# Loading the gathers' block numbers into registers for several query blocks at once

## The chip, the cores and the metric

One core of one Trainium2 chip. The metric is the device time of one execution of the kernel in microseconds. Three runs of the kernel before took 892.53, 896.0 and 898.25 us, median 896.0 us.

## What is computed

Block-sparse attention and, on its result, a bilinear feed-forward layer. There are 4 batches of 8 heads, 768 positions, head width 64. Positions form 24 blocks of 32. A query block attends to its two neighbours and itself, to block 0, to block 23 and to three sampled blocks; query blocks 0 and 23 attend to everything.

```python
scores = scale * np.matmul(q, k.transpose(0, 1, 3, 2))
...
for qb in range(n_blocks):
    for kb in sampled_blocks[qb]:
        mask[qb * block:(qb + 1) * block, kb * block:(kb + 1) * block] = True
scores = np.where(mask, scores, -1000000000.0)
...
return (a * b @ w_out).astype(np.float32)   # a = x @ w_a, b = x @ w_b
```

The sampled block numbers are an input (24 x 3 integers), so the kernel reads them at run time.

## The kernel before

**Tiling.** The 3072 tokens form 12 chunks of 256 (three for each batch; the first batch takes its middle chunk first, so its order of query blocks is 8 to 15, 0 to 7, 16 to 23). Each chunk has 8 query blocks. Of 96 query blocks 88 are sparse (1 to 22 of each batch) and 8 are dense (0 and 23). For a sparse one TensorE forms scores against 8 gathered key blocks (lines 976 and 875, tile `s`), VectorE finds the maximum (line 991), ScalarE the exponentials (line 1001, tile `sm`), both split the result into two half-precision parts (lines 893 to 900, tile `hl`), SyncE's queue transposes those by DMA (line 1023; line 1118 for dense ones; tile `pt`), and TensorE multiplies by the gathered values (line 919, tile `av`). When all 8 blocks of a chunk are done and scaled (lines 1163 and 1166, tile `xT`), the chunk goes through the feed-forward layer: first products `ab` (line 1202, 24 matmuls of 128x256 a step, 12 steps a chunk), their product and its split (lines 1219 to 1249), second products `o` (lines 1283 to 1285). The weights are unpacked and split during the first part of the span, by VectorE (lines 727 to 768) and ScalarE.

**The gathers.** For a sparse query block keys come by GpSimd copies inside the on-chip memory (`gather_keys`): one copy of the three neighbour blocks (line 586), now and then two of the blocks 0 and 23, and three copies of 128x128 words at offsets held in registers (line 591), into one of two buffers `KG`. Values come by DMAs on SyncE's queue (`gather_values`): one of three blocks (line 621), now and then two more (lines 623, 624), and three whose source address is held in a register (line 626), into one of two buffers `VG`. The offsets were clamped and multiplied by VectorE into two small tables, `offs` for values and `offs_k` for keys (lines 424 to 433). Ahead of the three register-addressed operations of every sparse query block, `dynamic` (line 563) loads that block's three offsets from the table into three registers of the queue that will use them. It is one instruction, TENSOR_LOAD, at line 566, on SyncE's queue for values and on GpSimd's queue for keys.

**What sets the order.** Every engine runs its instructions in program order, and that order is fixed when the kernel is built, by a planner in the kernel's own code (class `Plan`). Each piece of work is a generator that yields steps with an engine, a cost in ns and a rank; the planner keeps the time at which each engine, the DMA queue and the descriptor generator come free by these costs, and issues the step that can begin first, weighed by rank (attention by its query block, weights from 8 on, the feed-forward layer 8000 and more, so it fills). A step of `gather_values` costs SyncE 3000 ns in the plan, 1250 ns more with the two extra DMAs, 475 ns for a dense block (line 631). For a step with its last field set, as this one, the planner also holds the descriptor generator for the step's cost (line 159), and loads on ScalarE's queue wait for that one too. A step of `gather_keys` costs GpSimd 2000 ns (line 595). Nothing on the chip rereads these costs: they act only through the order of each engine's program.

Of the kernel before, what the change touches and what calls it, by code (L numbers as in the profile page):

```python
# [13 lines left out]
I32 = mybir.dt.int32  # L14
AF = mybir.ActivationFunctionType
ALU = mybir.AluOpType
PSUM = bass.MemoryType.PSUM

NB = 24
# [24 lines left out]
SM_BUFS = 3  # L44
LATE = 8
HL_BUFS = 3
GROUPS = ((0, 6), (6, 9), (9, 12))
G_LOW = float(2.0 ** 12)

# [167 lines left out]
Way = namedtuple("Way", "eng ns fn moved extra", defaults=(0, 0))  # L217
# [6 lines left out]
def dve(ns, fn):  # L224
    return [Way("DVE", ns, fn)]
# [20 lines left out]
def kernel(  # L246
# [12 lines left out]
    nc = tc.nc  # L259
    B, NCH, D, H, CH = q.shape  # L260
    NF, P, DM = w_a.shape
    S = NCH * CH
# [3 lines left out]
    BLK = S // NB  # L266
# [6 lines left out]
    NR = sampled_blocks.shape[1]  # L273
    ROW = 2 * H * D

    const = ctx.enter_context(tc.tile_pool(name="const", bufs=1))
# [10 lines left out]
    def take(tag, bufs):  # L287
        return rings.setdefault(tag, Ring(bufs)).take()
# [36 lines left out]
    w3 = const.tile([P, NF], F32, name="w3")  # L325
    w3_max = const.tile([P, len(GROUPS) + 1], F32, name="w3_max")
    vv = const.tile([P, B], F32, name="vv")
    unit = const.tile([P, NC + len(GROUPS)], F32, name="unit")
    to_g = const.tile([P, NC + len(GROUPS)], F32, name="to_g")
    to_out = const.tile([P, NC + len(GROUPS)], F32, name="to_out")  # L330
    junk = const.tile([P, KT * CH], BF16, name="junk")

    ident = const.tile([P, NB], BF16, name="ident")
    mrows = const.tile([P, 8, BLK], BF16, name="mrows")
    offs = const.tile([1, NB, 4], I32, name="offs")
    offs_k = const.tile([1, NB, 4], I32, name="offs_k")

    k_ready = [Event(NG) for _ in range(B)]
    k_scale = [Event(NG) for _ in range(B)]
# [18 lines left out]
    for b, i in units:  # L358
        dense = i in (0, NB - 1)
# [6 lines left out]
    w_bound = [Event(3) for _ in range(NF)]  # L366
    w_known = [Event(hi - lo) for lo, hi in GROUPS]
    all_known = Event(len(GROUPS))
    w_scale = [Event() for _ in range(NF)]
# [27 lines left out]
    def make_tables():  # L397

        box = work.tile([P, DM], F32, tag="st", name="mbox", bufs=ST_BUFS)
        held = yield from take("st", ST_BUFS)  # L400
        row = work.tile([P, DM], F32, tag="st", name="mrow", bufs=ST_BUFS)
        held2 = yield from take("st", ST_BUFS)
        sb = box[:NB, 0 : 2 * NR].bitcast(I32).rearrange("p (a b) -> p a b", b=2)
        cb = box[:NB, 8 : 8 + 5 + NB]
        sv = box[:NB, 40:48]
        eq = box[:NB, 48:56]
        dup = box[:NB, 56:64]
        one = row[0:1, 0 : 2 * NR * NB].bitcast(I32).rearrange("p (a b) -> p a b", b=2)
        clamped = row[0:1, 256 : 256 + NR * NB]
        clamped3 = clamped.rearrange("p (a b) -> p a b", b=NR)  # L410

        def load():
            nc.scalar.dma_start(
                one.rearrange("p a b -> p (a b)"),
                sampled_blocks.bitcast(I32).rearrange("(o a) b -> o (a b)", o=1),
            )
            nc.scalar.dma_start(
                sb.rearrange("p a b -> p (a b)"), sampled_blocks.bitcast(I32)
            )
            nc.scalar.dma_start(cb, c_blocks)  # L420

        yield [Way("ACT", 300, load, 250)]

        def starts():
            nc.vector.tensor_scalar(
                clamped, one[:, :, 0], 0.0, float(NB - 1), ALU.max, ALU.min
            )
            nc.vector.tensor_scalar(
                offs[:, :, :NR], clamped3, float(BLK), None, ALU.mult
            )  # L430
            nc.vector.tensor_scalar(
                offs_k[:, :, :NR], clamped3, float(BLK // 2), None, ALU.mult
            )

        t = yield dve(700, starts)
        tables.fire(t)
        held2.fire(t)

        def doubles():
            nc.vector.tensor_copy(sv[:, 0:5], cb[:, 0:5])  # L440
            nc.vector.tensor_scalar(
                sv[:, 5:8], sb[:, :, 0], 0.0, float(NB - 1), ALU.max, ALU.min
            )
            nc.vector.memset(ident, 0.0)
            nc.vector.memset(mrows, 0.0)
            nc.vector.tensor_copy(ident[:NB], cb[:, 5 : 5 + NB])
            nc.vector.memset(dup, 0.0)
            for s in range(3, 8):
                nc.vector.tensor_scalar(
                    eq[:, :s], sv[:, :s], sv[:, s : s + 1], MASKED, ALU.is_equal, ALU.mult  # L450
                )
                nc.vector.tensor_reduce(
                    dup[:, s : s + 1], eq[:, :s], axis=mybir.AxisListType.X, op=ALU.min
                )
            nc.vector.tensor_copy(mrows[:NB], dup.unsqueeze(2).to_broadcast([NB, 8, BLK]))

        t = yield dve(2300, doubles)
        held.fire(t)
        mask_ready.fire(t)


    def gate(i):
        if i >= 0:
            yield s_sent[units[i]]
# [96 lines left out]


    def dynamic(engine, table, i):
        eng = {"SP": mybir.EngineType.SP, "POOL": mybir.EngineType.Pool}[engine]
        step, top = (BLK, S - BLK) if table is offs else (BLK // 2, (S - BLK) // 2)
        return nc.values_load_multi_w_load_instructions(
            table[0:1, i, :NR], engines=(eng,), min_val=0, max_val=top,
            skip_runtime_bounds_check_because="the table is clamped to these bounds",
        )[1]

    def gather_keys(n):
        b, i = sparse[n]
# [26 lines left out]
    def gather_values(n):  # L599
        b, i, x = vg_units[n]  # L600
        yield from gate(order[b, i] - GATE_G)
        yield tables
        yield v_stored[b]
        vg_free[n] = yield from take("vg", VG_BUFS)
        if n + 1 < len(vg_units):
            plan.start(gather_values(n + 1), order[vg_units[n + 1][:2]] - LEAD_G)
        to = VG[n % VG_BUFS]
        first = n < VG_BUFS or vg_units[n - VG_BUFS][0] != b or vg_units[n - VG_BUFS][1] in (0, NB - 1)

        def copies():  # L610
            if i in (0, NB - 1):
                hq, x1 = divmod(x, 2)
                nc.sync.dma_start(
                    to.rearrange("p a x -> p (a x)")[:, : 3 * ROW // HQ].rearrange(
                        "p (t x) -> p t x", t=3
                    ),
                    vd[b][x1 * HALF : (x1 + 1) * HALF, hq * ROW // HQ : (hq + 1) * ROW // HQ]
                    .rearrange("(t p) x -> p t x", p=P),
                )
                return  # L620
            nc.sync.dma_start(to[0 : 3 * BLK, 0, :], vd[b][(i - 1) * BLK : (i + 2) * BLK, :])
            if first:
                nc.sync.dma_start(to[3 * BLK : P, 0, :], vd[b][0:BLK, :])
                nc.sync.dma_start(to[0:BLK, 1, :], vd[b][(NB - 1) * BLK :, :])
            for r, at in enumerate(dynamic("SP", offs, i)):
                nc.sync.dma_start(
                    to[(1 + r) * BLK : (2 + r) * BLK, 1, :], vd[b][bass.ds(at, BLK), :]
                )

        dense = i in (0, NB - 1)  # L630
        t = yield [Way("SP", 475 if dense else 3000 + 1250 * first, copies, 1300, 1)]
        vg_ready[b, i, x].fire(t + LATE_VG)

    kg_free, vg_free = {}, {}
# [307 lines left out]
    def turn(tag, b, i, hq=0):  # L942

        n = order[b, i]
        if hq == 0 and n > 0:
            i1 = units[n - 1][1]
            last = (tag, n - 1, HQ - 1 if i1 in (0, NB - 1) else 0)
        else:
            last = (tag, n, hq - 1)
        if n + hq > 0:  # L950
            yield turns.setdefault(last, Event())
        return turns.setdefault((tag, n, hq), Event())
# [6 lines left out]
    def attend(b, i):  # L959
# [50 lines left out]
        mine = yield from turn("hl", b, i)  # L1010
        gone = yield from take("hl", HL_BUFS)
        mine.fire(0)
        hl = work.tile([P, 2, HQ, NK], F16, tag="hl", name=f"hl{n}", bufs=HL_BUFS)
        for hq in range(HQ):
# [38 lines left out]
    def attend_quad(b, i, hq, ends):  # L1053
# [53 lines left out]
        for x in range(2):  # L1107
            gone = yield from take("hl", HL_BUFS)
            if x == 1:
                mine.fire(0)  # L1110
            hl = work.tile([P, 2, HALF], F16, tag="hl", name=f"hl{n}_{hq}{x}", bufs=HL_BUFS)
            t = yield from in_parts(sms[x], hl[:, 0], hl[:, 1], d1, HALF, False)
# [299 lines left out]
```

## Time and profile before

| what | value |
|---|---|
| runs, median (lowest to highest) | 896.0 us (892.53 to 898.25) |
| profiled execution, its time | 893.5 us |
| its span, first to last instruction | 891.7 us |
| granted TensorE clock, mean share of full speed | 0.985 |
| TensorE matmuls busy | 754.8 us, 85% |
| VectorE busy | 590.1 us, 66% |
| ScalarE busy | 490.6 us, 55% |
| GpSimd busy | 185.7 us, 21% |

The span is what the profiler recorded between the first and the last instruction; the execution's own time is 1.8 us longer. SyncE has no row in the table because everything it does is issuing, which the profile does not count as busy; its instructions have starts and lengths all the same. In the rows below, PE is TensorE, DVE VectorE, ACT ScalarE, POOL GpSimd and SP SyncE; a q behind the name is the engine's instruction queue. An arrow in a wait reads "waited for".

### The profile page before, as it was taken

The numbers are of one execution on the slowest core, as the hardware profiler recorded it, in microseconds if no ns is written. First come the engines' busy times: TensorE is split into PE (matmuls) and PEld (weight loads), VectorE is DVE, ScalarE is ACT, GpSimd is POOL, SyncE is SP. The second block draws the span as 40 slices with busy tenths as digits, with TensorE's granted clock in tenths as the row PEclk, the third lists the DMA queues.
The fourth block names the chain that finished last, engine by engine and source line by source line (L and its number), as shares of the span: only waits on it lengthen the run. The fifth ranks groups of instructions, "written<-read, shape, count | busy, mean of one in ns | idle before, by whom it ended". The sixth has DMA issues, their size and how long they took to land.

```text
span 891.7 us, 23906 instructions
## 1 busy us (share of the span) xinstructions
PE 754.8 (85%) x9024; PEld 557.1 (62%) x9024; DVE 590.1 (66%) x1600; ACT 490.6 (55%) x1174; POOL 185.7 (21%) x428
## 2 busy tenths in 40 slices
PE   0123488659999989799999989999999999999998
PEld 0112355447776767577777667667777767777775
DVE  3888989998657768476577766855676765342222
ACT  4676677688546457474475665843656544232222
POOL 0622233241113332130043331200332310000000
PEclk9999999979999999999999999999999999999999
DMA  9879997879568698967686699675857636341000
GB/s 253 276 178 229 249 225 210 233 181 214 149 148 178 131 153 213 196 152 183 140 172 158 149 212 203 147 173 142 172 132 162 144 92 153 81 122 28 25 1 24
DMA packets 209725, 142.35 MB, mean 160 GB/s; under 512 B 152649, under 2 KB 177226, under 8 KB 209610
## 3 DMA queue, kind: packets, MB, share of 16 engines
q1 hardware_dynamic: 197824, 103.07, 53.1%
q10 hardware_dynamic: 11786, 37.76, 13.8%
q8 instruction: 71, 1.16, 0.5%
q14 instruction: 44, 0.36, 0.1%
HBM read 86.25 MB, written 12.58 MB: 111 GB/s over the span
## 4 chain that ended last, share of the span: by engine, by line
PE 56%; DVE 17%; DMA 13%; ACT 5%; issue 4%; SPq 2%; POOL 1%; ACTq 0%; POOLq 0%; DVEq 0%
PE ab L1202 31%; PE av L919 5%; PE o L1283 5%; PE o L1285 5%; PE o L1284 5%; DMA pt<-hl 4%; PE s L875 3%; DMA q<-in_q_dram 2%; DMA keysT<-ks 2%; DVE hl L900 2%; DVE xT L1166 2%; DMA VG<-vd 1%; DVE QT L667 1%; DVE low L991 1%; DVE w L731 1%
## 5 line engine op out<-in xcount | busy, mean ns | idle before, releaser
L1202 PE MATMUL ab<-xT,wab 128*128 128x256 f16 x3456 | 408.6, 276 | 12.9 <-DVE a L1222 7.5
L1202 PEld LDWEIGHTS <-wab 128*128 128x128 f16 x3456 | 337.5, 99 | 79.2 <-issue 20.6
L1222 DVE SCALAR_TENSOR_TENSOR a<-a,to_g,ab 128x256 f32<-128x256 f32 x144 | 68.6, 478 | 123.2 <-ACT a L1219 121.7
L1219 ACT ACTIVATE a<-ab,w 128x256 f32<-128x256 f32 x144 | 67.5, 469 | 135.5 <-PE ab L1202 132.1
L586 POOL COPY KG<-keysT 128x384 int32<-128x384 int32 x88 | 64.5, 733 | 322.5 <-PE s L875 291.9
L919 PEld LDWEIGHTS <-VG 128*128 128x128 f16 x2688 | 98.8, 101 | 41.1 <-issue 19.8
L1001 ACT ACTIVATE sm<-s,low,cq 128x256 f32<-128x256 f32 x176 | 97.8, 558 | 47.4 <-DVE low L994 26.2
L1283 PE MATMUL o<-woh,gh 128*128 128x512 f16 x288 | 110.5, 384 | 14.8 <-ACT gh L1246 14.7
L919 PE MATMUL av<-pt,VG 128*128 128x64 f16 x2688 | 105.0, 197 | 21.2 <-DMA pt<-hl 9.7
L900 DVE SCALAR_TENSOR_TENSOR hl<-sm,den,hl 128x256 f16<-128x256 f32 (+1 forms) x208 | 105.7, 516 | 14.1 <-ACT hl L893 11.9
L1285 PE MATMUL o<-wos,gl 128*128 128x512 f16 x288 | 110.3, 383 | 4.5 <-DVE gl L1249 4.1
L1284 PE MATMUL o<-wol,gh 128*128 128x512 f16 x288 | 109.9, 382 | 0.0
L591 POOL COPY KG<-keysT 128x128 int32 x264 | 90.9, 382 | 37.6 <-POOL KG L586 23.2
L1246 ACT ACTIVATE gh<-a 128x256 f16<-128x256 f32 x144 | 59.4, 413 | 59.3 <-DVE a L1222 57.0
L1249 DVE SCALAR_TENSOR_TENSOR gl<-gh,a 128x256 f16<-128x256 f16 x144 | 63.5, 442 | 35.4 <-ACT gh L1246 34.2
L976 PE MATMUL s<-mrows,ident 128*32 128x192 bf16 (+1 forms) x352 | 25.8, 282 | 58.6 <-ACT sm L1001 32.0
L875 PE MATMUL s<-KG,QT 128*32 128x256 f16 x1408 | 59.8, 294 | 15.4 <-DMA QT<-QT 14.8
L1166 DVE SCALAR_TENSOR_TENSOR xT<-av,xT 64x256 f16<-64x256 f32 x96 | 40.4, 421 | 41.1 <-ACT xT L1163 38.7
L875 PEld LDWEIGHTS <-QT 128*32 128x32 f16 x1664 | 44.0, 102 | 28.9 <-issue 24.0
L991 DVE TENSOR_REDUCE low<-s 128x2 f32<-128x512 f32 x88 | 59.9, 681 | 1.7 <-PE s L875 1.2
L896 DVE TENSOR_SCALAR hl<-sm,den 128x256 f16<-128x256 f32 (+1 forms) x124 | 45.1, 367 | 22.6 <-DMA pt<-hl 22.3
L893 ACT ACTIVATE hl<-sm,den 128x256 f16<-128x256 f32 (+1 forms) x84 | 42.8, 521 | 26.1 <-DMA pt<-hl 20.7
(108 smaller groups left out, 719.6 us busy)
## 6 DMA issues: line engine op xcount, KB each, us to landing
VG<-vd SPq DMA_DIRECT2D x284, 64.0 KB, 2.3
VG<-vd SPq DMA_DIRECT2D x88, 192.0 KB, 2.9
VG<-vd SPq DMA_DIRECT2D x32, 384.0 KB, 3.7
q<-in_q_dram ACTq DMA_DIRECT2D x24, 256.0 KB, 5.9
QT<-QT SPq DMA_DIRECT2D x24, 256.0 KB, 3.1
vd<-vs SPq DMA_DIRECT2D x16, 384.0 KB, 3.6
out_dram<-ou SPq DMA_DIRECT2D x24, 256.0 KB, 2.3
stage<-in_k_dram ACTq DMA_DIRECT2D x12, 384.0 KB, 4.5
```

The lines of the kernel that those rows point to most:

```text
L591: nc.gpsimd.tensor_copy(to[:, :, (5 + r) * w : (6 + r) * w], of[:, :, bass.ds(at, w)])
L875: mm(to[h * BLK : (h + 1) * BLK], q_block(cc, i, 4 * hq + h, a), rhs(4 * hq + h), start=(first and a == 0), stop=(a == 1), skip_group_chec ...
L900: t = yield dve(221 + n * 1.03, lambda: nc.vector.scalar_tensor_tensor(lo, sm, over, hi, ALU.mult, ALU.subtract))
L919: mm(av[:, g, i % 2, :], w, pt[:, y, cols], start=(i % 2 == 0 and g == 0 and first and n + m == 0), stop=(last and n == len(terms) - 1 and ...
L991: yield dve(685, lambda: nc.vector.tensor_reduce(mx, ps, axis=mybir.AxisListType.X, op=ALU.max, negate=True))
L1001: t = yield act(750, lambda hq=hq: nc.scalar.activation(sm[:, hq], ps[:, hq], AF.Exp, bias=low[:, at, hq, 0:1], scale=cq[:, cc, hq : hq + ...
L1202: mm(ab[:, i, :], wab[:, f, i, part, kt, :], xc[:, kt, a, :], start=(i == 0 and kt == 0 and part + a == 0), stop=(kt == KT - 1 and a == 1) ...
L1219: yield act(470, lambda: nc.scalar.activation(a_sb, ab[:, 0, :], AF.Copy, scale=w3[:, f : f + 1]))
L1222: t = yield dve(420, lambda: nc.vector.scalar_tensor_tensor(a_sb, a_sb, to_g[:, n : n + 1], ab[:, 1, :], ALU.mult, ALU.mult))
L1283: mm(po, gh[:, js], woh[:, f, :], start=(f == lo), stop=False)
L1284: mm(po, gh[:, js], wol[:, f, :], start=False, stop=False)
L1285: mm(po, gl[:, js], wos[:, f, :], start=False, stop=(f == hi - 1))
```

## The change

`dynamic` keeps a list of held registers for each of the two queues. When the query block is 1, 8, 12 or 16 of its batch, one TENSOR_LOAD fetches the offsets of all query blocks up to the next of these numbers (7, 4, 4 and 7 blocks, 21, 12, 12 and 21 values); other query blocks take their three registers from the list. The tables lose their fourth, unused column so that several rows are contiguous. In the plan, `gather_values` costs 2250 ns in place of 3000, and 1200 ns more where it carries a load. The plan's cost of `gather_keys` stays at 2000 ns.

```diff
+LOADS = (1, 8, 12, 16)
...
-    offs = const.tile([1, NB, 4], I32, name="offs")
-    offs_k = const.tile([1, NB, 4], I32, name="offs_k")
+    offs = const.tile([1, NB, NR], I32, name="offs")
+    offs_k = const.tile([1, NB, NR], I32, name="offs_k")
...
     def dynamic(engine, table, i):
-        eng = {"SP": mybir.EngineType.SP, "POOL": mybir.EngineType.Pool}[engine]
-        step, top = (BLK, S - BLK) if table is offs else (BLK // 2, (S - BLK) // 2)
-        return nc.values_load_multi_w_load_instructions(
-            table[0:1, i, :NR], engines=(eng,), min_val=0, max_val=top,
-            skip_runtime_bounds_check_because="the table is clamped to these bounds",
-        )[1]
+
+        held = held_offsets[engine]
+        if i in LOADS:
+            eng = {"SP": mybir.EngineType.SP, "POOL": mybir.EngineType.Pool}[engine]
+            top = S - BLK if table is offs else (S - BLK) // 2
+            end = min([g for g in LOADS if g > i] + [NB - 1])
+            values = nc.values_load_multi_w_load_instructions(
+                table[0:1, i:end].rearrange("o a b -> o (a b)"), engines=(eng,),
+                min_val=0, max_val=top,
+                skip_runtime_bounds_check_because="the table is clamped to these bounds",
+            )[1]
+            for n in range(end - i):
+                held[i + n] = values[n * NR : (n + 1) * NR]
+        return held.pop(i)
+
+    held_offsets = {"SP": {}, "POOL": {}}
...
-        t = yield [Way("SP", 475 if dense else 3000 + 1250 * first, copies, 1300, 1)]
+        t = yield [Way("SP", 475 if dense else 2250 + 1250 * first + 1200 * (i in LOADS), copies, 1300, 1)]
```

## Rows read from the trace of the kernel before

**Rows 1.** busy time by engine in three stretches: start:end, length, busy us (instructions), granted clock, DMA.

```profile
core 0: us, PE busy (x) PEld busy (x) DVE busy (x) ACT busy (x) POOL busy (x), PEclk, DMA share, GB/s
...
0.00:200.00 200.00, 92.81 (x1192) 65.65 (x1193) 170.22 (x440) 135.20 (x310) 62.24 (x121) 0.96 0.87 226
...
200.00:790.00 590.00, 564.59 (x7021) 418.74 (x7020) 391.70 (x1098) 329.75 (x809) 123.09 (x306) 0.99 0.70 158
...
790.00:892.00 102.00, 97.44 (x815) 72.70 (x812) 28.15 (x64) 25.62 (x56) 0.36 (x1) 1.00 0.14 41
```

**Rows 2.** the same view, three stretches before 200 us.

```profile
40.00:120.00 80.00, 34.22 (x470) 24.69 (x470) 70.38 (x175) 55.30 (x137) 22.21 (x51) 1.00 0.91 221
...
120.00:200.00 80.00, 55.99 (x685) 39.20 (x683) 75.78 (x204) 58.31 (x137) 27.22 (x47) 0.91 0.82 215
...
176.00:190.00 14.00, 6.82 (x88) 5.38 (x87) 13.38 (x38) 10.36 (x28) 5.11 (x10) 0.63 0.43 122
```

**Rows 3.** what TensorE waited for, 0 to 200 us: total us, times, longest.

```profile
PE s L976 <- ACT sm L1001: 27.2, 7, 8.2
...
PE av L919 <- DMA VG<-vd: 8.5, 5, 2.9
...
PE av L919 <- DMA pt<-hl: 7.8, 3, 4.4
```

**Rows 4.** the same view, 200 to 790 us.

```profile
PE av L919 <- DMA pt<-hl: 1.9, 2, 1.5
...
PE av L919 <- DMA VG<-vd: 0.9, 2, 0.6
```

**Rows 5.** instructions of line 566: ns min/median/max, first to last start.

```profile
L566 SPq TENSOR_LOAD <-offs x88: 664/685/1953, 53.2 to 787.5; - x88
...
L566 POOLq TENSOR_LOAD <-offs_k x88: 726/732/2952, 29.2 to 723.2; - x88
```

**Rows 6.** SyncE's DMA issues in order of time: start, length, line; one gather.

```profile
305.00 0.34 SPq L621 DMA_DIRECT2D VG<-vd  x1
...
306.35 1.33 SPq L626 DMA_DIRECT2D VG<-vd  x3
```

**Rows 7.** GpSimd's first copy of a gather, line 586, ns min/median/max.

```profile
L586 POOL COPY KG<-keysT x88: 504/509/2472, 29.2 to 723.2; 128x384 int32<-128x384 int32 x88
```

**Rows 8.** what GpSimd's first copy waited for, whole span.

```profile
POOL KG L586 <- PE s L875: 291.9, 65, 51.3
```

**Rows 9.** chain that ended last, by line, in 28:62, 290:325 and 474:486 us.

```profile
by line: issue 40.0%; POOL KG L591 16.8%; DMA keysT<-ks 10.9%; POOLq L566 8.0%; PE s L875 5.7%; POOL KG L586 4.9%; POOL KG L589 4.5%; ACTq L711 2.0%; DVE hl L900 1.8%; POOL KG L588 1.8%; DVE low L991 1.8%; DVE w L731 1.7%; POOL power L384 1
...
by line: DMA pt<-hl 39.1%; SPq L626 8.3%; PE ab L1202 7.5%; SPq L566 6.2%; ACT QT L665 5.7%; issue 5.6%; DVE xT L1166 4.8%; ACT sm L1001 4.4%; SPq L1023 3.7%; DVE hl L900 2.5%; PE av L919 2.5%; DVE hl L896 2.3%; DVE low L991 2.0%; ACT xT L1
...
by line: DMA pt<-hl 34.4%; SPq L566 13.9%; SPq L626 10.0%; PE ab L1202 9.1%; issue 8.2%; DVE hl L900 7.2%; DVE hl L896 6.1%; PE s L875 3.9%; DVE gl L1249 2.8%; SPq L621 2.3%; PE s L976 1.6%; DVE low L994 1.4%; DVE low L991 0.6%
```

**Rows 10.** SyncE's DMA issues from 65 to 75 us.

```profile
65.11 0.54 SPq L621 DMA_DIRECT2D VG<-vd  x1
...
67.44 1.32 SPq L626 DMA_DIRECT2D VG<-vd  x3
...
69.39 5.44 SPq L1023 DMA_TRANSPOSE pt<-hl  x3
```

**Rows 11.** TensorE in order of time, with idle time before; near 74 and 183 us.

```profile
74.54 1.44 PE L919 MATMUL av<-pt,VG 128*128 128x64 f16 x24 [4.38 <-DMA pt<-hl]
...
183.18 0.35 PE L976 MATMUL s<-mrows,ident 128*32 128x192 bf16 x4 [8.15 <-ACT sm L1001]
```

**Rows 12.** what VectorE waited for, 40 to 200 us, the two longest.

```profile
DVE a L1222 <- ACT a L1219: 3.1, 1, 3.1
...
DVE power L387 <- POOL power L384: 3.0, 1, 3.0
```

More of the change, by code (lines that the diff above doesn't have):

```diff
@@ L428, in starts @@
             nc.vector.tensor_scalar(
-                offs[:, :, :NR], clamped3, float(BLK), None, ALU.mult
+                offs, clamped3, float(BLK), None, ALU.mult
             )
             nc.vector.tensor_scalar(
-                offs_k[:, :, :NR], clamped3, float(BLK // 2), None, ALU.mult
+                offs_k, clamped3, float(BLK // 2), None, ALU.mult
             )
```

## The prediction

> **What bounds the kernel now.** I read the busy times by stretch first. From 200 to 790 us TensorE is busy 564.59 of 590 us, and from 790 to 892 us 97.44 of 102 [rows 1]. Its work is fixed by the problem, so after 200 us the kernel is bound by TensorE, and all that any edit can win there is TensorE's idle time: 590 - 564.59 = 25.4 us, and 4.6 us at the end. Before 200 us TensorE is busy only 92.81 us [rows 1]: 107.2 us idle. There VectorE is the full engine, 70.38 and 75.78 us busy in the two stretches of 80 us [rows 2], because it unpacks the weights beside the first attention blocks.
>
> Second come TensorE's waits. Before 200 us it waited 8.5 us for gathered values and 7.8 us for transposed probabilities, both issued by SyncE, and 27.2 us for ScalarE to free a score bank [rows 3]. From 200 to 790 us the first two are only 1.9 and 0.9 us [rows 4]: SyncE's transfers are mostly early enough there, since the feed-forward products fill TensorE.
>
> Third, the chain of waits, for the loads that the change removes. They stand on it in three places [rows 9]: GpSimd's loads with 8.0% of the 34 us from 28 on, 2.7 us; SyncE's with 6.2% of the 35 us from 290 on, 2.2 us; and with 13.9% of the 12 us from 474 on, 1.7 us. Together 6.6 us.
>
> **What the change takes away and adds.** *Loads.* Each queue has 88 loads now [rows 5]. With it 4 a batch remain, 16; 72 go. On SyncE 72 x 0.685 = 49 us of queue time goes, on GpSimd 72 x 0.732 = 53 us (medians of rows 5). The three DMAs' address arithmetic stays: between the first DMA of a gather (305.00 + 0.34) and the next (306.35) lie 1.01 us [rows 6], of which the load is some 0.69, so about 0.3 us should be left.
>
> *The 16 larger loads.* They carry 21 or 12 values in place of 3, and no row shows one of that size. From below the cost is that of a load of three, 0.685 us. From above it is in proportion, 7 x 0.685 = 4.8 us and 4 x 0.685 = 2.7 us. The rows cannot part a fixed cost from one by value; they are nearest to the lower end, being loads themselves, and I take 1.2 us, the figure that the changed plan charges. Growth is then 16 x 0.5 = 8 us, and SyncE's net 49 - 8 = 41 us. Queued behind a load are its own three DMAs and then whatever the plan put next, transposes above all (at 69.39 us three of them, rows 10); for these TensorE waits.
>
> The shortest load of three values took 0.664 us here [rows 5]. The Trainium skill (DMA: Bandwidth & Descriptors, section Latency and other measured facts) gives a tensor load a floor of about 600 ns, which unrolling amortizes; by that page the large loads would stay near 0.69 us, and SyncE's net would be 49 us instead of 41. No run shown here has a large load, so the trace cannot confirm it.
>
> *GpSimd.* Its load runs beside the 0.509 us copy issued just before [rows 7], so some 0.732 - 0.509 = 0.22 us a gather is exposed, 72 x 0.22 = 16 us. But that copy waits 291.9 us in all for TensorE to free a key buffer [rows 8]: GpSimd is idle enough for this to count for nothing, except from 28 to 50 us, where gathers run end to end. If the cover were gone, the 16 us would be what counts.
>
> *Tables.* The same two VectorE instructions write as many values once; nothing, ahead of the first load at 29.2 us [rows 5].
>
> *What of this reaches the end.* After 200 us the 3.9 us of SyncE loads on the chain can return no more than the 1.9 + 0.9 = 2.8 us that TensorE waited for such transfers [rows 4]; what is late next is a feed-forward product on TensorE itself. I take 1 us. Before 200 us there are two places. GpSimd's 2.7 us from 28 on [rows 9]. And the gather at 65.11 us: its first DMA ends at 65.65, the next starts at 67.44 [rows 10], 1.79 us against 1.01, so its load held the queue some 1.5 us; behind it stand the transposes for which TensorE idled 4.38 us until 74.54 [rows 11]. That is 2.7 + 1.5 = 4.2 us, between 0 and the 8.5 + 7.8 = 16.3 us of rows 3. VectorE is 88% busy there and comes next; of its own waits the longest, 3.1 and 3.0 us, are for ScalarE and GpSimd, none for SyncE [rows 12]. So I take 3 of the 4.2 us. Sum: -1 - 3 = **-4 us**.
>
> *The plan's cost.* A step of SyncE is charged 750 ns less in 72 gathers and 450 ns more in 16: 54 - 7 = 47 us less planned SyncE and descriptor-generator time. This changes the programs of all five engines from the first gathers on, as the planner picks by who can begin first. No row prices a new order. From the side of gain: TensorE's waits for SyncE's transfers all go, 16.3 + 2.8 = 19 us, though before 200 us VectorE has just 160 - 70.38 - 75.78 = 13.8 us free between 40 and 200 us [rows 2]. From the side of loss: early holes such as the one of 8.15 us before 183.18 us [rows 11], with the clock at 0.63 of full in the 14 us around it [rows 2], are repeated. The old cost fitted the old gather (rows 6 span 2.7 us, plan 3.0) and the new one fits the new gather equally (2.0, plan 2.25), so nothing says that the plan becomes a better or worse description; I take 0 and keep both ends.
>
> **The number.** The profiled execution took 893.5 us, so 889.5 for it; the median of the runs shown is 2.5 us above it: **892 us**.
>
> **The rivals.**
> *1. Nothing arrives.* TensorE's 25.4 us of idle time are mostly waits for ScalarE and VectorE, VectorE holds the early stretch, and the 4 us are absorbed by what is late next: 896 us. For it speak rows 4, against it the loads on the chain [rows 9].
> The Trainium skill (Perfetto Trace Analysis, section Identifying the Most-Contended Engine) says that kernels gain mainly by improving the most contended engine; SyncE's loads are not on it after 200 us, and by that page the time would stay. The trace agrees there (564.59 of 590 us busy).
> *2. The new order fills the early holes.* With SyncE's queue shorter, transposes and gathers come in time for each early block, and attention of the first chunk, which gates the feed-forward layer, ends sooner. At most VectorE's 13.8 free us are used; with 1 us after 200, 896 - 14.8 = 881; I price it at 883 us. For it: 16.3 us of rows 3. Against: a VectorE that is 95% busy from 120 to 200 us.
> *3. Slower: scores queued too early on TensorE.* The plan believes that gathers land sooner, so it puts a block's scores earlier in TensorE's program, where the score bank is still being read by ScalarE; the in-order TensorE then stands, with feed-forward products behind. This wait is there now: 27.2 us in 7 places, 3.9 us each [rows 3], all before 200 us. Three more are +11.7 us, and one stretch at the lower level of the clock, 1.2 in place of 2.4 GHz, as in 176 to 190 us (0.63 of full over 14 us, so 14 x 0.37 = 5 us lost) makes +16.7; less the 4 us, 896 + 12.7 = 909 us. It decides from three more such holes; two without the clock (+7.8 - 4) are no difference. Against it: from 200 us on the product fill leaves that wait small.
> *4. Loads cost by value, or are split into several instructions.* Then queue time is not removed but lumped: four lumps a batch, two of them 4.8 us where the plan allows 1.2. The 8 lumps are 3.6 us late each, 29 us; before 200 us, with two or so of them, it is felt in full, later hardly: some +7 - 1, 902 us.
>
> **How the numbers follow.** About 1%, 9 us, is what a measurement of this kernel can tell from no change; so under 887 is faster, over 905 slower. Forecast 892: 0.37. Rival 1, 896: 0.16. Rival 2, 883: 0.27. Rival 3, 909: 0.15. Rival 4, 902: 0.05. The forecast's own edge below 887 adds 0.02 to faster, and rival 4's upper edge with the forecast's 0.02 to slower: faster 0.29, same 0.54, slower 0.17. The forecast's own range is 886 to 896. The range to hold 8 in 10 reaches down to 880, near the full 14.8 us of rival 2, and up to 906, so that most of rival 3 and a little below rival 2's price are left out.
>
> **What the changed profile would show.** Line of the loads: 16 on each queue, none near 4.8 us; if more than 16, or lengths in proportion to the values, rival 4. Between line 621 and the first of line 626 about 0.3 us instead of 1.01 in the gathers without a load. GpSimd's loads gone from the chain between 28 and 50 us. The waits of rows 3 for gathered values and transposes down from 16.3 to about 13 us, with busy time of TensorE before 200 us up by some 3 us: right. Unchanged there: rival 1. Down to a few us: rival 2. The wait for ScalarE's freeing of score banks above 27.2 + 11.7 = 39 us, or the granted clock from 120 to 200 us below 0.91: rival 3. What would make the forecast wrong is above all a change of TensorE's idle time before 200 us (107.2 us) in either direction by more than 10 us, with the loads themselves as foreseen.

## The result

The changed kernel takes 900.25 us in the median of 12 runs against 891.8 us for the kernel before on the same chip: ratio **1.0073**, 95% interval 1.0044 to 1.0103. It is slower by 0.7%, where 0.4% faster was forecast; the time lies inside the stated range, on the other side of no change. Ratios here leave out runs that lie over 1.5% above the fastest run of the same kernel, and so differ a little from ratios of the medians; the profiled execution of the changed kernel is such a run (906.4 us, the longest of the 12, span 904.6), so lengths of instructions and the order are read from its trace, and sums over the span only with care.

### The profile page after: what moved, and what is told of

Read it like the earlier page. It is cut to its first block, busy times and chain, and to the rows that moved or that the text cites. A ratio compares the mean times of both kernels' runs of the same rounds, so it can differ in the third digit from the quotient of the medians.

```text
span 904.6 us, 23778 instructions
## 1 busy us (share of the span) xinstructions
PE 761.4 (84%) x9024; PEld 559.2 (62%) x9024; DVE 588.1 (65%) x1595; ACT 493.7 (55%) x1179; POOL 186.1 (21%) x428
## 4 chain that ended last, share of the span: by engine, by line
PE 55%; DMA 13%; DVE 12%; ACT 7%; issue 6%; SPq 3%; POOL 2%; ACTq 0%; POOLq 0%; DVEq 0%
PE ab L1213 30%; PE av L930 6%; PE o L1294 5%; PE o L1296 5%; PE o L1295 5%; DMA q<-in_q_dram 3%; DMA pt<-hl 3%; PE s L886 3%; DMA VG<-vd 2%; DVE hl L911 2%; ACT sm L1012 2%; DVE xT L1177 1%; DMA keysT<-ks 1%; SPq L571 1%; DMA stage<-in_k_dram 1%
## 5 line engine op out<-in xcount | busy, mean ns | idle before, releaser
L1294 PE MATMUL o<-woh,gh 128*128 128x512 f16 x288 | 112.6, 391 | 21.2 <-ACT gh L1257 19.9
L930 PE MATMUL av<-pt,VG 128*128 128x64 f16 x2688 | 107.3, 199 | 27.3 <-DMA VG<-vd 9.5
L930 PEld LDWEIGHTS <-VG 128*128 128x128 f16 x2688 | 101.2, 102 | 44.4 <-issue 31.0
L597 POOL COPY KG<-keysT 128x384 int32<-128x384 int32 x88 | 55.5, 631 | 334.6 <-PE s L886 308.0
L1295 PE MATMUL o<-wol,gh 128*128 128x512 f16 x288 | 112.1, 389 | 0.0
L602 POOL COPY KG<-keysT 128x128 int32 x264 | 104.6, 436 | 33.0 <-issue 29.5
L1260 DVE SCALAR_TENSOR_TENSOR gl<-gh,a 128x256 f16<-128x256 f16 x144 | 64.5, 448 | 29.7 <-ACT gh L1257 28.8
L886 PE MATMUL s<-KG,QT 128*32 128x256 f16 x1408 | 59.5, 293 | 16.3 <-DMA QT<-QT 15.6
L886 PEld LDWEIGHTS <-QT 128*32 128x32 f16 x1664 | 44.0, 101 | 30.7 <-issue 25.4
L1294 PEld LDWEIGHTS <-gh 128*128 128x128 f16 x288 | 28.3, 98 | 50.5 <-ACT gh L1257 25.1
L987 PEld LDWEIGHTS <-ident 128*32 128x32 bf16 x352 | 10.8, 95 | 77.8 <-issue 47.5
```

The costliest lines, as they stand in the source:

```text
L602: nc.gpsimd.tensor_copy(to[:, :, (5 + r) * w : (6 + r) * w], of[:, :, bass.ds(at, w)])
L886: mm(to[h * BLK : (h + 1) * BLK], q_block(cc, i, 4 * hq + h, a), rhs(4 * hq + h), start=(first and a == 0), stop=(a == 1), skip_group_chec ...
L930: mm(av[:, g, i % 2, :], w, pt[:, y, cols], start=(i % 2 == 0 and g == 0 and first and n + m == 0), stop=(last and n == len(terms) - 1 and ...
L1260: t = yield dve(460, lambda: nc.vector.scalar_tensor_tensor(gl, gh, -G_LOW, a_sb, ALU.mult, ALU.add))
L1294: mm(po, gh[:, js], woh[:, f, :], start=(f == lo), stop=False)
L1295: mm(po, gh[:, js], wol[:, f, :], start=False, stop=False)
```

## The profile after

The busy times by stretch, columns as in [rows 1], and 120 to 200 us, as in [rows 2]:

```profile
0.00:200.00 200.00, 94.57 (x1187) 66.92 (x1188) 168.20 (x435) 139.08 (x317) 61.93 (x121) 0.93 0.89 225
200.00:790.00 590.00, 558.04 (x6904) 411.08 (x6903) 387.37 (x1087) 324.37 (x796) 123.83 (x306) 0.98 0.67 157
...
120.00:200.00 80.00, 57.38 (x637) 39.88 (x638) 73.19 (x200) 59.95 (x140) 24.12 (x47) 0.86 0.83 196
```

Before 200 us little has changed. After it TensorE is busy 558.04 us against 564.59 [rows 1], with 117 matmuls fewer (6904 for 7021): its idle time there went from 25.4 to 32.0 us. In this execution the loss is in the stretch where the forecast expected 1 us of gain.

The loads, line 571 now (ns min/median/max), answer to [rows 5]:

```profile
L571 POOLq TENSOR_LOAD <-offs_k x16: 805/1356/7812, 30.7 to 688.7; - x16
L571 SPq TENSOR_LOAD <-offs x16: 753/1236/4296, 55.2 to 753.5; - x16
```

There are 16 on each queue as meant, the median on SyncE is the 1.2 us that was taken, and the longest takes 4.30 us there and 7.81 us on GpSimd. The gathers without a load are as foreseen (SyncE's issues, one gather, against [rows 6]): 294.01 + 0.52 to 294.78 leaves 0.25 us where 1.01 stood.

```profile
294.01 0.52 SPq L632 DMA_DIRECT2D VG<-vd  x1
294.78 1.31 SPq L637 DMA_DIRECT2D VG<-vd  x3
```

What TensorE waited for, first before 200 us (against [rows 3]), then after it (against [rows 4]); total us, times, longest:

```profile
PE s L987 <- ACT sm L1012: 29.7, 8, 8.1
...
PE av L930 <- DMA pt<-hl: 8.0, 5, 3.9
...
PE av L930 <- DMA VG<-vd: 4.4, 3, 2.0
...
PE o L1294 <- ACT gh L1257: 11.5, 11, 3.9
PE av L930 <- DVE xT L1177: 6.9, 5, 1.6
PE av L930 <- DMA VG<-vd: 5.0, 2, 3.1
```

The same two waits in the kernel before, 200 to 790 us:

```profile
PE o L1283 <- ACT gh L1246: 7.5, 4, 5.6
...
PE av L919 <- DVE xT L1166: 2.0, 2, 1.6
```

Early, the waits for gathered values and transposes fell from 16.3 to 12.4 us. Later, the wait for gathered values rose from 0.9 to 5.0 us, and two waits that ScalarE and VectorE end, not SyncE, grew: that for the split of the feed-forward product (`gh`) from 7.5 to 11.5 us, and that for `xT` from 2.0 to 6.9 us.

One long load can be followed. The chain of waits around 446 us (start, length, what):

```profile
446.30 4.29 SPq L571
...
451.81 1.75 DMA VG<-vd
...
453.70 1.28 PE av L930 x21
```

This is the load for blocks 1 to 7 of a batch. It belongs to the first gather behind a dense block, and the chain runs from it through the gather's own DMAs straight to the value products, for which TensorE stood the 3.1 us of the wait above. On SyncE's queue that load takes 4.29 us in every batch. The load of blocks 16 to 22, with equally many values, takes 1.44 to 1.49.

So two suspects stand: the long load (theory A) and the new order of the programs (theory B).

## The experiments

Ratios are to the kernel before, run on the same chip in turn; in brackets the 95% interval.

**Loads and order apart.** *aligned*: the table in four groups, each starting at a multiple of 128 bytes, with the changed plan.

```diff
-    offs = const.tile([1, NB, NR], I32, name="offs")
+    offs = const.tile([1, len(LOADS), 32], I32, name="offs")
...
-                table[0:1, i:end].rearrange("o a b -> o (a b)"), engines=(eng,),
+                table[0:1, LOADS.index(i), : (end - i) * NR], engines=(eng,),
```

> The changed kernel with its table of offsets laid out by groups, each group's offsets starting at a multiple of 128 bytes, so that the load for blocks 1 to 7 no longer starts at byte 12 of the table; same loads, same plan. Theory A (the slow load at that start is the loss: 4.29 us of SyncE's queue in each batch, 12.9 us of the chain in three batches): the four loads fall to the 1.4 us that the other loads of 21 values took, GpSimd's from 5.6 to 7.8 us to 1.5 to 2.2 us, and the ratio to the kernel before falls from 1.007 to between 0.993 and 1.000. Theory B (the new order of the programs is the loss): ratio 1.004 to 1.007, whatever the loads take.

Measured: 1.0040 [1.0000, 1.0081]. The loads are cured (ns min/median/max):

```profile
L572 SPq TENSOR_LOAD <-offs x16: 764/1282/2125, 54.4 to 738.9; - x16
```

The time hardly follows: the interval overlaps that of the changed kernel. *plan_only*: the kernel before with the changed line of costs and nothing else.

> The kernel before with the changed plan's costs (2250 ns, 1200 more at blocks 1, 8, 12 and 16) and its 88 loads of three values on each queue as before. Theory A: the order is worth nothing by itself, ratio 0.998 to 1.003. Theory B: the order is the loss, ratio 1.005 to 1.010.

Measured: 1.0247 [1.0183, 1.0310]. The new order alone, with the old loads, costs far more than the whole change, and more than either theory foresaw. *loads_only*: the changed kernel with the old cost.

```diff
-        t = yield [Way("SP", 475 if dense else 2250 + 1250 * first + 1200 * (i in LOADS), copies, 1300, 1)]
+        t = yield [Way("SP", 475 if dense else 3000 + 1250 * first, copies, 1300, 1)]
```

> The changed kernel with the plan's old cost (3000 ns a gather), so the programs keep the order of the kernel before and only the loads differ. Theory A: loads at byte 12 still 4.29 us on SyncE's queue, ratio 1.004 to 1.012. Theory B: the order is the old one, ratio 0.995 to 1.000.

Measured: 1.0018 [0.9980, 1.0057], between the two theories. *aligned_oldplan*: both edits.

> The grouped, aligned table with the plan's old cost, so old order and cheap loads. Both theories: 0.993 to 0.999, by the 4 us that were foreseen; theory A expects it equal to the aligned kernel with the new plan, theory B some 0.7 per cent below that one.

Measured: 0.9921 [0.9878, 0.9965]. These four corners, two layouts by two orders, can be read as a square. With the old order the loads are worth -0.8% if aligned and nothing clear as the change lays them out. Alignment is worth 0.97% with the old order and 0.33% with the new one; the new order costs 1.19% with aligned loads and 0.55% with the loads as changed. Each of these differences is uncertain by 0.5 to 0.6%, so only the two large ones are clear of noise. Both theories hold a part; which is the larger depends on the one that is undone first.

**Why that load is long.** *shifts*: the aligned kernel with one table a batch, whose groups start 0, 4, 8 and 12 bytes late.

> The aligned table and the old plan's cost, with one copy of the tables for each batch; in batch b every group starts 4b bytes behind a multiple of 128 bytes (0, 4, 8 and 12 bytes). Only the lengths of the loads are read. Theory A1 (a load that starts off a multiple of 16 bytes is read in pieces): on SyncE's queue 21 values take 1.4 us in batch 0 and about 4.3 us in batches 1 to 3, and 12 values 0.76 us in batch 0 and some 2.1 to 2.9 us in the others. Theory A2 (only the byte 12 start of the changed kernel is bad, by where it lies to a 64 byte line): batches 1 and 2 stay at 1.4 us, batch 3 is slow. Theory A3 (it is the stretch of the program behind a dense block, not the address): all batches 1.4 us, or slow at block 1 alone.

Measured (SyncE's loads one by one; batch 0 with 12 and 21 values, batch 1 with 21 and 12):

```profile
L573 SPq TENSOR_LOAD <-offs x1: 776/776/776, 76.2 to 76.2; - x1
...
L573 SPq TENSOR_LOAD <-offs x1: 1449/1449/1449, 120.1 to 120.1; - x1
...
L573 SPq TENSOR_LOAD <-offs x1: 4292/4292/4292, 280.0 to 280.0; - x1
...
L573 SPq TENSOR_LOAD <-offs x1: 2497/2497/2497, 323.3 to 323.3; - x1
```

Batches 2 and 3 are as batch 1 (4.29 and 4.30 us for 21 values at block 1). So the price goes by the address, as theory A1 has it; that the load is read in pieces is not shown. A start off a multiple of 16 bytes costs about 0.20 us a value (4.29 / 21, 2.50 / 12), an aligned one next to nothing more for 12 values than for 3. Counted from the start of the table, in the changed kernel blocks 8, 12 and 16 start at bytes 96, 144 and 192, and block 1 at byte 12. The old table's rows of four words kept every start aligned; dropping the fourth column undid that.

**How the time follows the charge.** Aligned loads throughout, and against *aligned_oldplan* only the number in the plan differs, 2500, 2750, 3250, 3500 and 4250 for 3000 (the edit for 3500):

```diff
-        t = yield [Way("SP", 475 if dense else 3000 + 1250 * first, copies, 1300, 1)]
+        t = yield [Way("SP", 475 if dense else 3500 + 1250 * first, copies, 1300, 1)]
```

*cost2500*:

> Aligned loads, and the plan charges 2500 ns for every gather of values (no extra for a load). The old cost of 3000 gave 0.992, the changed one (2250 and 1200 at a load) 1.004. Theory T (slack: the lower the charge, the tighter the plan's order and the worse it runs, since a gather really lasts 2.1 us or more): between them, 0.996 to 1.002. Theory C (chance: any other charge gives another order, and the time scatters by a per cent with no trend): anywhere from 0.985 to 1.010.

*cost2750*:

> The same with 2750 ns. Theory T: 0.993 to 0.998, below the kernel with 2500. Theory C: no order by the charge.

*cost3250*:

> Aligned loads, 3250 ns charged for every gather of values. Theory T (slack in the charge): between 3000 (0.992) and 3500 (0.985), 0.986 to 0.992. Theory C (chance): anywhere from 0.980 to 1.005.

*cost3500*:

> The same with 3500 ns, above the old charge. Theory T: still 0.988 to 0.993, or slightly more where too much slack delays gathers. Theory C: no order by the charge, as likely 1.000 or more.

*cost4250*:

> The same with 4250 ns. Theory T: the gain flattens or turns, 0.980 to 0.992, since a charge of twice the real 2.1 us must delay gathers at some point. Theory C: anywhere from 0.980 to 1.005.

| charge, ns | ratio, aligned loads | ratio, loads of three values | ratio, loads as changed |
|---|---|---|---|
| 2250, 1200 more at a load | 1.0040 [1.0000, 1.0081] | 1.0247 [1.0183, 1.0310] | 1.0073 [1.0044, 1.0103] |
| 2500 | 0.9999 [0.9970, 1.0028] | | |
| 2750 | 0.9998 [0.9964, 1.0032] | | |
| 3000 | 0.9921 [0.9878, 0.9965] | 1 (the kernel before) | 1.0018 [0.9980, 1.0057] |
| 3250 | 0.9873 [0.9819, 0.9927] | | |
| 3500 | 0.9853 [0.9798, 0.9909] | 0.9809 [0.9761, 0.9857] | 0.9930 [0.9895, 0.9965] |
| 4250 | 1.0534 [1.0487, 1.0581] | | |

From 2250 to 3500 the time falls, or once stays, from each charge to the next in every column, which scatter by chance would hardly do over six, three and three points, though neighbouring intervals overlap. Theory T's ranges held at 2500 and 3250; 2750 came out above its range and 3500 below it. At 4250 the time jumps, outside both theories: there TensorE waits 11.3 us for gathered values from 200 to 790 us, where it was 0.9 us [rows 4]. The other two columns with 3500:

*before3500*, the kernel before with 3500 for 3000:

> The kernel before, with its 88 loads of three values on each queue, and 3500 ns charged in place of 3000. If loads and charge add up (loads worth 0.8 per cent, charge from 3000 to 3500 worth 0.7): 0.990 to 0.996. If the charge only helps where it exceeds the real gather, which lasts 3.06 us here: 0.994 to 1.000. If all of the gain at 3500 is the charge's: 0.983 to 0.988.

It measured 0.9809 [0.9761, 0.9857], better than any of the three: at that charge the large loads bring nothing.

*after3500*, the changed kernel with 3500:

> The changed kernel as it is, its load of blocks 1 to 7 at byte 12 included, with 3500 ns charged in place of 2250 and 1200. If the charge is the larger loss: 0.986 to 0.996, that is 0.985 as with aligned loads and up to 1 per cent for the slow loads. If the slow loads bind in this order too: 0.996 to 1.004.

*after3500b*, the same again:

> The changed kernel with 3500 ns charged, a second time: four of its first six runs lay over 1.5 per cent above the fastest, so its ratio of 0.980 rests on two, and the median of all six stands at 0.995. If the slow loads of blocks 1 to 7 cost nothing in this order: 0.978 to 0.988. If they cost what they cost with the old order, about 1 per cent: 0.990 to 0.998.

The first gave 0.9802 [0.9715, 0.9889], which rests on two runs; the second, resting on ten, gave 0.9930 [0.9895, 0.9965]. By that one the misaligned loads still cost 0.8% against aligned ones (0.9853).

**What carries the charge.** *sp_only*: 3500 ns for SyncE, the descriptor generator held for 2250 only.

```diff
-            self.generator = at + (625 if turn else way.ns if way.extra else 455)
+            self.generator = at + (625 if turn else way.ns + way.extra - 1 if way.extra else 455)
...
-        t = yield [Way("SP", 475 if dense else 3000 + 1250 * first, copies, 1300, 1)]
+        t = yield [Way("SP", 475 if dense else 3500 + 1250 * first, copies, 1300, 1 if dense else -1249)]
```

> Aligned loads, 3500 ns charged to SyncE, but the descriptor generator held for 2250 ns only, so loads on ScalarE's queue are planned as with the changed kernel's charge. If the slack works through SyncE's queue: 0.983 to 0.990, as with 3500 for both. If it works through the generator, which ScalarE's loads share: 0.997 to 1.004, as with 2250.

Measured: 0.9760 [0.9713, 0.9807], 870.99 us in the median, the fastest here. It works through SyncE's queue. That it beats 3500 for both was not expected; that the longer hold of the generator costs something would fit it, but no run isolates this.

*turnpad*: the changed charge, but the plan holds SyncE 1250 ns longer after another step, the transposes of sparse blocks.

```diff
-                self.free[way.eng] = max(at + 625, start + max(way.moved - 952, -125) + 25)
+                self.free[way.eng] = max(at + 625, start + max(way.moved - 952, -125) + 25) + 1250 * (way.ns == 1300)
```

> Aligned loads and the changed kernel's charge for gathers (2250, 1200 more at a load), but the plan holds SyncE 1250 ns longer after the transposed probabilities of each sparse query block. Per block SyncE's planned time is then that of the 3500 ns charge. Theory Q (what counts is how long SyncE's queue is held in the plan for each block, whichever step is charged): 0.975 to 0.992. If the charge must stand on the gather itself: 1.000 or more.

Measured: 0.9802 [0.9757, 0.9847]. Against *aligned* one term of the plan differs, and 2.4% are gone. What counts is SyncE's planned time per query block, in both of the places where it was charged.

*late3750*: the changed charge and a planned latency.

```diff
-    LATE_PT, LATE_VG, LATE_AV, LATE_G = 2500, 2500, 1500, 700
+    LATE_PT, LATE_VG, LATE_AV, LATE_G = 2500, 3750, 1500, 700
```

> Aligned loads and the changed kernel's charge (2250, 1200 more at a load), but the plan takes gathered values to be usable 1250 ns later (LATE_VG 3750 in place of 2500). This delays the planned attention by a latency and leaves the queue's planned occupancy as it is. Theory P (what counts is that attention is not planned ahead of the feed-forward steps): 0.983 to 0.995, with fewer than 57 query blocks done at 500 us and TensorE's idle time after 200 us under 22 us. Theory Q (what counts is how long the gathers hold SyncE's queue in the plan): 1.000 to 1.008, as without it.

Measured: 1.0119 [1.0078, 1.0159], worse than either theory: a planned latency of 1250 ns does not do what 1250 ns of planned occupancy do. *gate3*: gathers let go one block later (`GATE_G` 3 for 4).

> Aligned loads, the changed kernel's charge, and gathers let go only when the scores three query blocks earlier are sent, in place of four. Theory P (attention planned too far ahead of the feed-forward steps): 0.985 to 0.999. Theory Q: no gain, 1.000 to 1.010, as SyncE's planned occupancy is unchanged.

Measured: 0.9991 [0.9959, 1.0023], 0.5% better than *aligned*, with intervals that overlap; it lies between the two theories and decides nothing. *vg3*: a third value buffer (`VG_BUFS` 3 for 2).

> Aligned loads, the changed kernel's charge, and a third buffer for gathered values, so that a gather at the head of SyncE's queue seldom waits for the value products to free one (up to 22.7 us in the aligned kernel). Theory H (those waits hold up the transposes behind and are the loss): 0.980 to 0.992. Theory P (attention planned ahead of the feed-forward steps is the loss): 0.998 to 1.012, as a further buffer lets attention run further ahead.

Measured: 1.0164 [1.0101, 1.0227], outside both ranges. The edit did not do what it was for, though. What the first DMA of a gather waited for at the head of SyncE's queue (line 633 in sparse blocks, 625 in dense ones; whole span, total us, times, longest), in *aligned* and then in *vg3*:

```profile
SPq L633 <- PE av L931: 127.4, 34, 22.7
...
SPq L625 <- PE av L931: 19.8, 15, 4.8
...
SPq L625 <- PE av L931: 77.1, 20, 21.7
SPq L633 <- PE av L931: 63.4, 18, 22.1
```

That is 147.2 us in all before and 140.5 after, with waits as long as before, so theory H was not tested. It stays a rival. The longest wait of a sparse gather for a value buffer is 18 to 25 us in every kernel that charges the gather 3000 ns or less, *turnpad* apart, and it is 15.0 us in *cost3250*, 8.2 in *cost3500*, 7.6 in *before3500*, 9.0 in *sp_only* and 4.9 in *turnpad*. Up to 3500 ns the long waits and the lost time go away together; whether one causes the other is not shown.

**What the charge does on the chip.** Theory P can be held against counts, each from one execution: in the first 500 us, the matmuls of `av` (28 a query block on average) and of `ab` (24 a feed-forward step). The columns are busy us (instructions) of TensorE, VectorE and ScalarE on that tile, then granted clock and DMA. The kernel before, `av` and then `ab`:

```profile
0.00:500.00 500.00, 62.59 (x1536) 21.90 (x52) 19.48 (x52) 0.97 0.80 192
...
0.00:500.00 500.00, 191.67 (x1587) 30.95 (x65) 30.41 (x65) 0.97 0.80 192
```

*before3500*:

```profile
0.00:500.00 500.00, 62.08 (x1532) 21.80 (x52) 19.42 (x52) 0.96 0.81 191
...
0.00:500.00 500.00, 198.16 (x1656) 32.46 (x68) 31.65 (x68) 0.96 0.81 191
```

The same for more runs, with TensorE's busy time from 200 to 790 us, in order of the ratio:

| run | ratio | `av` by 500 us | `ab` by 500 us | TensorE busy, us of 590 |
|---|---|---|---|---|
| *turnpad* | 0.9802 | 1560 | 1658 | 577.16 |
| *before3500* | 0.9809 | 1532 | 1656 | 577.49 |
| *cost3500* | 0.9853 | 1536 | 1662 | 574.38 |
| *aligned_oldplan* | 0.9921 | 1584 | 1632 | 569.10 |
| *gate3* | 0.9991 | 1608 | 1551 | 562.88 |
| the kernel before | 1 | 1536 | 1587 | 564.59 |
| *aligned* | 1.0040 | 1608 | 1556 | 563.15 |
| *late3750* | 1.0119 | 1584 | 1512 | 559.58 |
| *plan_only* | 1.0247 | 1584 | 1522 | 558.96 |
| *cost4250* | 1.0534 | 1409 | 1512 | 541.46 |

So the loss goes with TensorE's idle time after 200 us, and the feed-forward layer is what falls behind. Theory P (attention planned too far ahead, so that feed-forward steps are missing as fill) fits the step from 2250 to 3500 ns: attention in *aligned* is 72 matmuls ahead of *cost3500*, and the feed-forward layer 106 behind, over four steps of 2.62 us. It does not fit the step from 3000 to 3500: the kernel before and *before3500* are level in attention (1536 and 1532), yet 69 `ab` matmuls and 1.9% apart. *late3750* has less attention done than *aligned* and is slower, and *cost4250* has the least and is the slowest. Attention running ahead is thus not the cause in general.

That the charge sets the time is shown by the one-number edits. By which wait it does so stays open. The two waits named above go part of the way with it: `av` for `xT` is 5.9 us in *plan_only* and 6.9 in *aligned*, and 2.0, 1.6 and 1.6 in the kernel before, *cost3500* and *before3500*; `o` for `gh` is 12.9, 8.8, 7.5, 5.4 and 4.1 us in the same five. No run forces one of these, or the long waits of the gathers, alone.

## Why the prediction was wrong

**The step that failed** is "so nothing says that the plan becomes a better or worse description; I take 0". The new cost is as true as the old one was, as the text said: a gather without a load lasts 2.1 us in the median against 2.25 charged. It is wrong all the same, since the true cost is not the best one to plan with. By the square, the order costs 1.2% with aligned loads (10.6 us of some 892) and 0.55% with the loads as changed (4.9 us), and by *plan_only* 2.5% with small loads (22 us). Of the ends that the text kept, -19 us here and +16.7 us in rival 3 hold the first two and not the third; the value between them was chosen from an argument on truthfulness that no row supported.

**The second step that failed** is on the tables, "the same two VectorE instructions write as many values once; nothing". Written as cheaply, yes, but the narrower rows moved block 1 to byte 12. Four loads a queue grew, on SyncE from 1.44 to 4.29 us, 4 x 2.85 = 11.4 us of queue time, and on GpSimd to 5.6 to 7.8 us; which queue's loads cost the time was not tried apart. With the old order 8.7 us reached the end (1.0018 - 0.9921), give or take 5. The upper bound, 4.8 us in proportion to the values, was almost the price of these four; the other twelve took 0.75 to 1.49 us, around the 1.2 us that was taken.

**The direct gain** was right in sign and undersized: -4 us foreseen, -7 us (0.9921, from -11 to -3) with aligned loads and the old order. It lay elsewhere, though. In the trace of *aligned_oldplan* TensorE has done 39 matmuls more than before by 200 us (1231 against 1192 [rows 1]) and 65 more from 200 to 790 us (7086 against 7021, busy 569.10 us against 564.59, 4.5 us more). So of the 3 + 1 us split the larger part comes late, where rows 4 allowed at most 2.8. One reading, not tested, is that the wait rows bound what a transfer holds up directly, not what an earlier transfer lets others do.

**The sum.** Forecast were -4 us for the loads, 0 for the tables and 0 for the order; the square, taken in that order, gives -7, +8.7 and +4.9, together +6.5 us, each with some 5 us of uncertainty. That the time still lies in the stated range is the width of the range and errors of both signs, not the mechanism.

**Foreseen and seen:** 0.25 us left between the DMAs of the gather shown (0.3); early waits for SyncE's transfers at 12.4 us (13); GpSimd's loads gone from the chain between 28 and 62 us. Not seen: TensorE's busy time before 200 us up by 3 us; it rose by 1.8 us at a lower granted clock (0.93 against 0.96), with 5 matmuls fewer.

**The rivals.** Rival 3 had the right side and the right cause, the plan, but the wrong place: score-bank waits before 200 us went from 27.2 to 29.7 us, far from the 39 that it asked, and what grew were other waits, after 200 us. (The prediction has that wait all before 200 us; in the kernel before 4.9 us more of it lie between 200 and 790 us.) Its second sign came true, a granted clock of 0.86 from 120 to 200 us against 0.91, but this sign does not tell slow from fast: the clock there is 0.84 in *cost3500* and 0.85 in *before3500*. Rival 4, held at 0.05, named 902 us, the nearest to the 900.25 measured, and in part for its reason: its lump came true for the load of blocks 1 to 7 alone, by the address first and only then by the count, and the order of the programs made up the rest.

By the Trainium skill (DMA: Bandwidth & Descriptors, section Latency and other measured facts) a load has a floor near 600 ns; no load here was shorter than 0.66 us, so the traces agree. That large loads would stay near 0.69 us was the prediction's own step from it: 12 aligned values do (0.78 us in the row shown), 21 aligned (1.44) and misaligned ones (2.50 and 4.29) do not. The Trainium skill's rule to improve the most contended engine first (Perfetto Trace Analysis, section Identifying the Most-Contended Engine) was read in rival 1 as leaving the time alone. The runs do not bear that reading out: edits to the planned time of SyncE moved the time from 0.976 to 1.053, by way of TensorE's own idle time.

## What to carry to other kernels

Where a planner's costs fix the programs, an edit that "only updates the cost" is a new program on every engine: measure it apart from the edit that it accompanies, and sweep it, since the best cost may lie well above the true one (3.25 to 3.5 us charged for 2.1 here). Where an edit is to take a wait away, look in its trace whether the wait is gone before its time is used for or against the wait. Keep what a register load reads on multiples of 16 bytes; a padding column that looks unused may be what does so.

## What was not expected of the hardware

A load of registers from on-chip memory costs on SyncE's queue 0.69 us for 3 values (median), from 0.75 us for 12 and from 1.44 us for 21 when it starts at a multiple of 16 bytes, and from 2.48 us for 12 and 4.29 for 21 otherwise. In the changed kernel the last is the same to 1% in all four batches; the others are at times longer, a load of 3 values by up to 1.3 us. On GpSimd's queue the misaligned load of 21 took 5.6 to 7.8 us in the changed kernel, and aligned ones 1.53 to 3.80 us in *aligned*.
